# Two small steps of the second head pair's row sums, moved from GpSimd to ScalarE and VectorE

## The chip, the cores and the metric

The kernel runs on one NeuronCore of a Trainium2 chip. The metric is the device time of one execution in microseconds, the median of several runs; lower is better. The engines are named as in the profile: PE is TensorE (PEld its weight loads), DVE is VectorE, ACT is ScalarE, POOL is GpSimd, and SP is SyncE, which issues most of the DMAs. Each engine works through its own instructions in program order, and semaphores hold an instruction until what it reads is there.

## The reference

The reference is attention with rotary embedding, then a top-1 mixture of experts, then a dense layer pair with softplus between. Only the attention is touched by the change. Cut to that:

```python
q_rot, k_rot = (rotate(q), rotate(k))            # 2 batches x 8 heads, 576 positions, 64 wide
scores = scale * np.matmul(q_rot, k_rot.transpose(0, 1, 3, 2))
scores = scores - np.max(scores, axis=-1, keepdims=True)
attn = np.exp(scores)
attn = attn / (np.sum(attn, axis=-1, keepdims=True) + 1e-09)
out = np.matmul(attn, v)
```

The addition of `1e-09` to the row sums is the guard addition of this document.

## The kernel before

The 16 heads of the attention run as 8 pairs, numbered j = 0 to 7 (heads 2j and 2j+1); the second pair is j = 1. A row of a head is a query position. Of the 576 rows of a head four blocks of 128 are full and 64 are left over; the left-over rows of both heads of a pair share one block. So a pair has nine blocks, numbered g = 0 to 8, of which g = 4 is the shared one, and the attention has 72 blocks. The loop at line 753 takes one step t for each block, with j and g from `divmod(t, 9)`.

In a step the order of each engine's work is written by hand (the scheduler is switched off). ACT takes the exponentials of block t, and with them adds up its rows into the tile `rst` of the head (`softmax_exp`, L543). PE transposes block t-1 (L549), multiplies the scores of block t+2 (L533), and does the filling work of the step: the products with v (`pv`, L597 to L599), the transposes that prepare the next pair's q and k (L446 and L450, into `pt`), those of a block's 64 left-over columns (`tail`, L581), and a head's output transposed back (`xout`, L616, into `px`). DVE takes the row maxima of block t+1 (L537) and the low parts of the transposed block t-2 (`ev_lo`, L567). ACT copies the high parts of block t-1 (`ev_hi`, L556). Last in the step comes what was put into the list `late`, the latest entry first. Among it is the second half of `xout`, on DVE: the reciprocal of the row sums (L621), then two products that empty the `px` bank (L623 into `zp`, L628 into `xrow`).

The banks `pt`, `tail`, `px` and `po` come from one PSUM pool with two buffers (`ps_m`, tag "m"). A bank that PE wants to write must have been emptied: the `pt` that follows a `tail` in the first step of a pair takes the bank of the `px` before it.

The row sums of a head go through `ev_lo`. After the shared block (g = 4) the sums of the odd head's left-over rows, which lie in the even head's tile, are copied to the odd head's tile (L562). After g = 4 and after g = 8 the guard is added, for the even and for the odd head, into the tile `rinv` (L572 on GpSimd, or L574 on ScalarE). In the kernel before, pair 0 has these steps on VectorE and ScalarE, and the pairs 1 to 7 have them on GpSimd.

GpSimd does mainly the rotation of the pairs to come. In pair j the generator `rope_gen(j + 2)` gives it, step by step, the products with cosine and sine (L379, L381), sums (L389), and the split of k and of v into high and low parts (L412, L414, L396, L394). The small steps on the row sums stand between these in its queue.

Of the kernel before, what the change touches and what calls it, by code (L numbers as in the profile page):

```python
# [25 lines left out]
P = 128  # L26
# [4 lines left out]
LEFT = S - NC4 * P  # L31
# [59 lines left out]
def f(ap):  # L91
    return ap.bitcast(F32)
# [3 lines left out]
def moe_kernel(ctx: ExitStack, tc: tile.TileContext, q, k, v, emb, tau, w1, w2, w_in, w_out, rope, tab, out):  # L96
    nc = tc.nc
    V, A, G, T, SY = nc.vector, nc.scalar, nc.gpsimd, nc.tensor, nc.sync
# [220 lines left out]
    with actx:  # L319
# [178 lines left out]
        def head(i):  # L498
            if i not in heads:
                heads[i] = dict(a=i % 2, rst=rs[i % 3])  # L500
            return heads[i]

        def columns(hd):

            if 'ph' not in hd:
                hd['ph'], hd['pl'] = (hp.tile([P, 4, S], F32R, tag=n, name=n) for n in ("ph", "pl"))
            return hd
# [7 lines left out]
        def where(t):  # L515

            j, g = divmod(t, 9)
            return j, g, ([(2 * j + g // 5, g % 5)] if g != 4 else [(2 * j, 4), (2 * j + 1, 4)])
# [39 lines left out]
        def ev_lo(t):  # L558
            j, g, hs = where(t)
            tp = tiles.pop(('tp', t))  # L560
            if g == 4:
                (G if j else V).tensor_copy(head(2 * j + 1)['rst'][0:LEFT, 4:5], head(2 * j)['rst'][LEFT:P, 4:5])  # L562
            for x, (i, c) in enumerate(hs):
                w = P // len(hs)
                hd = columns(head(i))
                sl = slice(c * P, c * P + w)
                V.tensor_tensor(hd['pl'][:, :, sl], tp[:, :, x * w:x * w + w], f(hd['ph'][:, :, sl]), op=ALU.subtract)  # L567
            if g in (4, 8):
                hd = head(2 * j + g // 8)
                ri = hd['ri'] = small.tile([P, 5], F32, tag="rinv", name="rinv")  # L570
                if j:
                    G.tensor_scalar(ri, hd['rst'][:, 0:5], 1e-9, None, op0=ALU.add)  # L572
                else:
                    A.activation(ri, hd['rst'][:, 0:5], AF.Copy, bias=1e-9)  # L574
# [178 lines left out]
        for t in range(NS + 5):  # L753
            j, g = divmod(t, 9)
# [54 lines left out]
            if 2 <= t < NS + 2:  # L809
                ev_lo(t - 2)  # L810
# [668 lines left out]
```

## Time and profile before

| | us |
|---|---|
| runs: median (lowest to highest of 3) | 575.5 (575.0 to 577.9) |
| the profiled execution | 576.86 |
| its span, first to last instruction | 575.1 |
| PE busy | 545.2 |
| DVE busy | 447.0 |
| ACT busy | 439.0 |
| POOL busy | 203.3 |

The span is 1.8 us shorter than the time of the profiled execution, which itself is 1.4 us above the median of the runs. The attention takes about the first 187 us, the experts go on to about 365 us, and the dense pair ends the kernel. PE is busy for 95% of the span. The page also gives the clock that TensorE was granted, as a share of full speed, in 40 slices of 14.4 us.

A timeline row reads: start, duration, engine, line, operation, what it writes and reads, its shape, and how often it stands there in a run; in brackets the idle time of the engine ahead of it and what ended this.

### The profile page before, as it was taken

To read this page: it belongs to the slowest core of one execution; us is meant where nothing else is said; L and a number is where in the kernel's file an instruction comes from. 1 tells how busy PE (TensorE), PEld (TensorE's weight loads), DVE (VectorE), ACT (ScalarE), POOL (GpSimd) and SP (SyncE) were. 2 spreads that over 40 slices of the span, in tenths; PEclk is the share of its full clock that TensorE was granted. 3 is DMA by queue.
4 is the path that set the end of the run, shared out by engine and by line. 5 is a ranking of instruction groups with operands and counts; after the bars stand their busy time and mean duration, and the time that the engine had idled before them with its cause. 6 is when DMAs were issued, how large, how long until landed. Compare 5 with 4: busy or idle time off the path is not lost. (4 is left out here: it accounts for less than half of the span.)

```text
span 575.1 us, 10070 instructions
## 1 busy us (share of the span) xinstructions
PE 545.2 (95%) x3361; PEld 478.9 (83%) x3361; DVE 447.0 (78%) x741; ACT 439.0 (76%) x838; POOL 203.3 (35%) x317
## 2 busy tenths in 40 slices
PE   6889899999998899999999999998999999999995
PEld 6789899999888788887777888886889999888994
DVE  5797688787977679989999999687877766787243
ACT  3788688877875599789988998788878877677550
POOL 7999999839931330332222311200000000000033
PEclk9999899999999999999999999999999999999998
DMA  5434100051143635892539895373332222000012
GB/s 142 112 96 121 33 0 2 2 199 58 38 137 146 190 130 166 303 350 77 172 123 319 296 382 196 92 220 108 109 99 85 75 74 75 35 1 1 1 74 91
DMA packets 38631, 70.90 MB, mean 123 GB/s; under 512 B 9506, under 2 KB 25250, under 8 KB 38448
## 3 DMA queue, kind: packets, MB, share of 16 engines
q1 hardware_dynamic: 35600, 62.95, 33.2%
q0 software_dynamic: 2800, 7.09, 3.6%
q8 instruction: 28, 0.46, 0.3%
q10 hardware_dynamic: 176, 0.18, 0.2%
q14 instruction: 27, 0.22, 0.1%
HBM read 91.14 MB, written 8.13 MB: 173 GB/s over the span
## 5 line engine op out<-in xcount | busy, mean ns | idle before, releaser
L970 DVE TENSOR_TENSOR wt<-raw,wt 128x1024 fp32r<-128x1024 f32 x100 | 116.3, 1219 | 5.2 <-ACT wt L966 5.1
L1340 PE MATMUL ph<-yt,wt 128*128 128x320 f32 (+1 forms) x576 | 105.5, 336 | 2.7 <-ACT r__5875 L1352 1.8
L1340 PEld LDWEIGHTS ph<-yt,wt 128*128 128x128 f32 x576 | 93.5, 188 | 12.2 <-ACT r__5875 L1352 2.3
L1387 PE MATMUL po<-wt,g 128*128 128x512 f32 x432 | 103.6, 391 | 0.0
L966 ACT CAST wt<-raw 128x1024 fp32r<-128x1024 f32 x100 | 98.9, 1066 | 5.4 <-DMA raw<-in_moe_w_dram 5.4
L1387 PEld LDWEIGHTS po<-wt,g 128*128 128x128 f32 x432 | 80.4, 188 | 16.7 <-ACT g L1371 0.3
L1034 PE MATMUL py<-wt,ht 128*128 128x512 f32 x312 | 75.7, 395 | 3.6 <-DVE wt L970 3.6
L1404 POOL DMA_INDIRECT out_dram<-acc,otok x9 | 9.6, 1067 | 186.2 <-DVE acc L1401 185.6
L1034 PEld LDWEIGHTS py<-wt,ht 128*128 128x128 f32 x312 | 57.5, 188 | 16.3 <-DVE wt L970 4.9
L1005 PE MATMUL ph<-wt,xt 128*128 128x512 f32 x288 | 69.1, 394 | 0.0
L543 ACT ACTIVATE p<-sc,nm 128x576 f32<-128x576 f32 x72 | 54.0, 750 | 12.5 <-DVE nm L537 11.9
L1005 PEld LDWEIGHTS ph<-wt,xt 128*128 128x128 f32 x288 | 53.1, 188 | 10.6
L537 DVE TENSOR_REDUCE nm<-sc 128x1 f32<-128x576 f32 x72 | 54.1, 753 | 5.5 <-PE sc L533 4.3
L556 ACT CAST ph<-tp 128x512 fp32r<-128x512 f32 (+1 forms) x80 | 42.8, 547 | 12.9 <-PE tp L549 12.5
L533 PE MATMUL sc<-kt,qt 128*128 128x288 f32 x256 | 51.1, 323 | 1.6 <-ACT p L543 1.0
L567 DVE TENSOR_TENSOR pl<-tp,ph 128x512 fp32r<-128x512 f32 (+1 forms) x80 | 49.4, 627 | 0.0
L379 POOL TENSOR_TENSOR t<-qk,ropet 128x256 f32<-128x256 f32 x61 | 43.8, 746 | 11.1 <-DMA qk<-in_q_dram 10.7
L549 PE MATMUL tp<-idf,p 128*128 128x128 f32 x288 | 44.6, 278 | 1.9 <-DVE jz L233 0.6
L1371 ACT CAST g<-e 128x512 fp32r<-128x512 f32 (+2 forms) x33 | 21.6, 658 | 29.7 <-PE po L1387 20.2
L1372 DVE TENSOR_TENSOR g<-e,g 128x512 fp32r<-128x512 f32 (+2 forms) x33 | 24.3, 740 | 23.7 <-ACT g L1371 23.5
L533 PEld LDWEIGHTS sc<-kt,qt 128*128 128x128 f32 x256 | 37.4, 195 | 2.9 <-ACT p L543 1.9
L597 PE MATMUL po<-ph,vs 128*128 128x288 f32 x128 | 36.8, 309 | 2.7 <-DVE p L435 1.5
(245 smaller groups left out, 1002.4 us busy)
## 6 DMA issues: line engine op xcount, KB each, us to landing
raw<-in_moe_w_dram SPq DMA_DIRECT2D x116, 512.0 KB
raw<-in_moe_w_in_dram SPq DMA_DIRECT2D x16, 512.0 KB
raw<-in_moe_w_out_dram SPq DMA_DIRECT2D x16, 512.0 KB
yr<-ys SPq DMA_DIRECT2D x9, 256.5 KB
qk<-in_k_dram SPq DMA_DIRECT2D x8, 256.0 KB
qk<-in_q_dram SPq DMA_DIRECT2D x8, 256.0 KB
vv<-in_v_dram SPq DMA_DIRECT2D x8, 256.0 KB
xs<-xrow SPq DMA_DIRECT2D x1, 1024.0 KB
```

The source lines that it names most:

```text
L379: eng.tensor_tensor(t[:, i, g], x4[:, i, g], ropet[:, m, 0:4].unsqueeze(2).to_broadcast([P, 4, 2, 32]), op=ALU.mult)
L533: T.matmul(sc[:, n, 0:288], lhsT=w, rhs=r, start=(x == 0), stop=(x == len(mm) - 1))
L537: V.tensor_reduce(nm, tiles['sc', t][:, :, 0:288], axis=AX.XY, op=ALU.max, negate=True)
L543: A.activation(p.rearrange("p (n t) -> p n t", n=2), tiles.pop(('sc', t))[:, :, 0:288], AF.Exp, bias=tiles.pop(('nm', t)), accum_out=head( ...
L549: T.transpose(tp[:, x], p[:, x * P:x * P + P], idf)
L567: V.tensor_tensor(hd['pl'][:, :, sl], tp[:, :, x * w:x * w + w], f(hd['ph'][:, :, sl]), op=ALU.subtract)
L966: A.copy(wt[:, 0], raw)
L970: (eng or V).tensor_tensor(wt[:, 1], raw, f(wt[:, 0]), op=ALU.subtract)
L1005: T.matmul(ph[i], lhsT=xt[:, a, c], rhs=wt[:, r, 512 * i:512 * i + 512] if n else wt[r][:, 512 * i:512 * i + 512], start=(c == 0 and a == ...
L1034: T.matmul(py, lhsT=ht[c // 2][:, a, k], rhs=rhs[:, s], start=(c == 0 and r == 0 and a == 0 and s == 0), stop=(c == 3 and r == 1 and a == 1))
L1340: T.matmul(phs[i][:, 0:n1 - n0], lhsT=wt[:, a, k], rhs=yts[p][:, r, k, n0:n1], start=(k == 0 and a == 0 and r == 0), stop=(k == 3 and a == 1))
L1387: T.matmul(outs[i][c], lhsT=g[:, a, c * P:c * P + P], rhs=wt[:, r], start=(first and a == 0 and r == 0), stop=(last and a == 1))
```

## The change

In the two conditions of `ev_lo` the pair number from which the steps go to GpSimd rises by one: pair 1 now has them where pair 0 has them.

```diff
             if g == 4:
-                (G if j else V).tensor_copy(head(2 * j + 1)['rst'][0:LEFT, 4:5], head(2 * j)['rst'][LEFT:P, 4:5])
+                (G if j > 1 else V).tensor_copy(head(2 * j + 1)['rst'][0:LEFT, 4:5], head(2 * j)['rst'][LEFT:P, 4:5])
...
-                if j:
+                if j > 1:
                     G.tensor_scalar(ri, hd['rst'][:, 0:5], 1e-9, None, op0=ALU.add)
                 else:
                     A.activation(ri, hd['rst'][:, 0:5], AF.Copy, bias=1e-9)
```

Three instructions change their engine; PE and SP keep theirs as they were. In the rows below `rs0`, `rs1` and `rs2` are the three tiles of row sums, which the heads take in turn (head 2 has `rs2`, head 3 has `rs0`), and `rinv` is the sums with the guard added.

On POOL, at the end of the split of k for pair 3:

```order
 L412 CAST ks_849<-t1_676 128x9x64
 L414 TENSOR_TENSOR ks_849<-t1_676,ks_849 128x9x64
-L562 COPY rs0_99<-rs2_101 64x1
-L572 TENSOR_SCALAR rinv_877<-rs2_101 128x5
 L396 CAST vs_679<-vv_634 128x4x64
 L394 TENSOR_TENSOR vs_679<-vv_634,vs_679 128x4x64
```

The copy of the last sums and head 2's guard addition no longer stand behind the split of k; head 3's addition, 11 rows further on, goes as well.

On ACT, in step t = 15 (the seventh block of pair 1), for head 2:

```order
 L604 COPY ot0_142<-po_831 128x288
 L434 CAST p4_817<-po_831 64x2x64
+L574 ACTIVATE rinv_877<-rs2_101 128x5
 L556 CAST ph_846<-tp_856 128x4x128
 L543 ACTIVATE p_883,rs0_99<-sc_826,nm_872 128x576
```

Head 2's addition now stands ahead of the copy of the high parts of block 14. Head 3's stands in the same way in step t = 19, between the casts of `qt` and `ph`.

On DVE, in step t = 15:

```order
 L567 TENSOR_TENSOR pl_714<-tp_789,ph_713 128x4x128
 L537 TENSOR_REDUCE nm_872<-sc_826 128x1
+L562 COPY rs0_99<-rs2_101 64x1
 L567 TENSOR_TENSOR pl_714<-tp_821,ph_713 128x4x64
 L567 TENSOR_TENSOR pl_847<-tp_821,ph_846 128x4x64
```

The copy of the last sums now stands between the row maxima of block 16 and the low parts of block 13.

## Rows read from the trace of the kernel before

**Rows 1.** The page: busy time and share of engines; granted clock, tenths, 40 slices.
```profile
PE 545.2 (95%) x3361; PEld 478.9 (83%) x3361; DVE 447.0 (78%) x741; ACT 439.0 (76%) x838; POOL 203.3 (35%) x317
...
PEclk9999899999999999999999999999999999999998
```

**Rows 2.** Stretches: length, each engine's busy time, granted clock, DMA share, GB/s.
```profile
56.00:58.00 2.00, 1.44 (x13) 1.16 (x11) 0.00 (x1) 1.49 (x4) 1.86 (x2) 1.00 0.58 171
58.00:60.00 2.00, 0.39 (x3) 0.42 (x4) 1.29 (x4) 0.29 (x1) 1.76 (x5) 0.94 0.12 26
60.00:62.00 2.00, 2.00 (x11) 2.00 (x10) 1.97 (x4) 1.07 (x2) 1.84 (x5) 0.50 0.00 0
62.00:64.00 2.00, 2.00 (x13) 2.00 (x13) 1.52 (x3) 0.85 (x3) 1.92 (x4) 0.71 0.50 137
```

**Rows 3.** Timeline of DVE around 58 us.
```profile
55.32 0.68 DVE L567 TENSOR_TENSOR pl<-tp,ph 128x512 fp32r<-128x512 f32 x1
58.57 0.19 DVE L621 RECIPROCAL rinv<-rinv 128x5 f32<-128x5 f32 x1 [2.57 <-POOL rinv L572]
...
58.98 0.48 DVE L628 TENSOR_TENSOR xrow<-px,rinv 128x320 f32<-128x320 f32 x1
```

**Rows 4.** Timeline of POOL in the same stretch.
```profile
56.53 1.41 POOL L414 TENSOR_TENSOR ks<-t,ks 128x576 fp32r<-128x576 f32 x1
58.01 0.18 POOL L562 COPY rs<-rs 64x1 f32<-64x1 f32 x1
58.28 0.26 POOL L572 TENSOR_SCALAR rinv<-rs 128x5 f32<-128x5 f32 x1
58.60 0.40 POOL L396 CAST vs<-vv 128x256 fp32r<-128x256 f32 x1
...
63.91 0.23 POOL L572 TENSOR_SCALAR rinv<-rs 128x5 f32<-128x5 f32 x1
```

**Rows 5.** Timeline of PE in the same stretch.
```profile
54.74 1.30 PE L616 MATMUL px<-xm,ot 128*128 128x72 f32 x10
...
56.84 0.60 PE L581 MATMUL tail<-idf,p 128*64 128x128 f32 x4
59.61 0.97 PE L450 MATMUL pt<-idf,qq 128*128 128x128 f32 x4 [2.17 <-DVE xrow L628]
```

**Rows 6.** Stretches from the middle of one pair to the next, columns as in rows 2.
```profile
46.95:70.45 23.50, 21.14 (x162) 20.37 (x161) 16.60 (x31) 16.66 (x42) 22.50 (x36) 0.93 0.28 79
70.45:90.62 20.17, 19.77 (x161) 18.80 (x161) 16.37 (x32) 16.49 (x42) 19.16 (x33) 1.00 0.00 1
90.62:110.82 20.20, 19.82 (x162) 18.85 (x161) 16.38 (x32) 16.48 (x42) 18.34 (x30) 1.00 0.01 2
```

**Rows 7.** Timeline of DVE: the subtraction after block g = 4 of pairs 1 and 2.
```profile
46.95 0.68 DVE L435 TENSOR_TENSOR p<-tail,p 64x512 fp32r<-64x512 f32 x1 [1.72 <-ACT p L434]
...
70.45 0.69 DVE L435 TENSOR_TENSOR p<-tail,p 64x512 fp32r<-64x512 f32 x1 [1.72 <-ACT p L434]
```

**Rows 8.** Timelines of ACT and DVE in pair 0, which has the steps there.
```profile
28.28 0.20 ACT L574 ACTIVATE rinv<-rs 128x5 f32<-128x5 f32 x1
28.38 0.57 ACT L556 CAST ph<-tp 128x512 fp32r<-128x512 f32 x1
...
28.29 0.15 DVE L562 COPY rs<-rs 64x1 f32<-64x1 f32 x1
```

**Rows 9.** Timelines of POOL, DVE and PE: the same place in pair 2.
```profile
75.95 0.23 POOL L572 TENSOR_SCALAR rinv<-rs 128x5 f32<-128x5 f32 x1
...
79.39 0.18 DVE L621 RECIPROCAL rinv<-rinv 128x5 f32<-128x5 f32 x1
...
80.76 0.60 PE L450 MATMUL pt<-idf,qq 128*128 128x128 f32 x4
```

**Rows 10.** Timeline of PE: two later pauses.
```profile
196.75 0.54 PE L984 MATMUL pt<-idr,xg 128*128 128x128 f32 x4 [1.51 <-DMA xg<-xs,idx]
...
390.93 3.03 PE L1340 MATMUL ph<-yt,wt 128*128 128x512 f32 x12 [1.83 <-ACT r__5875 L1352]
```

## The prediction

> **What bounds the kernel now.** I read the page first: PE is busy for 95% of the span and its granted clock is at full speed in nearly all slices, but the fifth slice (57.5 to 71.9 us) shows an 8 [rows 1]. So the first question was what PE lacks in that slice. Cut into stretches of 2 us, it shows PE busy for 1.44 and then 0.39 of 2 us, and right after that a granted clock of 0.50, which is the lower of its two levels (1.2 instead of 2.4 GHz), until about 63 us [rows 2]. The reader is to see two losses there that follow one another: a pause, and then work at half clock.
>
> Next I followed the pause back, engine by engine. PE ends the transposes of `tail` at 57.44 and starts those of `pt` at 59.61, a pause of 2.17 us that is put down to DVE's product L628 [rows 5]; `pt` needs the bank that L628 empties. DVE had ended its work at 56.00 and stood 2.57 us ahead of the reciprocal L621, for POOL's addition L572 [rows 3]. POOL did this addition from 58.28 to 58.54, directly behind the split of k for pair 3 and the copy L562 [rows 4]. DVE started 0.03 us after POOL's end, and what else DVE needs, the `px` products of PE, had ended by 56.04 [rows 5], so the wait is rightly named. The sums themselves had long been there: they belong to block g = 4, and the filling work of that block is seen on DVE at 46.95 [rows 7]. POOL was simply late with its queue.
>
> **What the pause costs in all.** I measure it from pair to pair, between the same instruction of two pairs: the subtraction L435 after block g = 4 starts at 46.95 in pair 1 and at 70.45 in pair 2 [rows 7]. That is 23.50 us, against 20.17 us and 20.20 us in the next two pairs, with practically the same number of instructions, all at full clock [rows 6]. The excess is 23.50 - 20.17 = 3.33 us. Of it 2.17 us are the pause, and the remaining 1.16 us are the half clock after it.
>
> The stretches give the clock's part in another way: at half speed PE ran for 0.24 us (of 58 to 60, from 0.94), 2.00 us, and 1.16 us (of 62 to 64, from 0.71), together 3.40 us [rows 2]. The page "TensorE: Matmul & The Clock Gate" of the Trainium skill (section "HAM oscillation") prices time at the lower clock at one minus the ratio of the clocks, here one half, which would be 1.70 us and a sum of 575.5 - 2.17 - 1.70 + 0.1 = 571.7 us. The pairs bear out only 1.16 us of it, and I go by them, since part of those 3.40 us went to waits that the slow clock hid.
>
> **The change, part by part.**
>
> 1. *The guard addition of head 2 goes to ACT, step 15.* It then stands ahead of a `ph` cast, in the seventh block of pair 1, some 6 us ahead of the reciprocal that needs it. Its price is in pair 0: the addition starts at 28.28 and the next cast at 28.38, so it takes 0.10 us of ACT's queue, although it lasts 0.20 us [rows 8]. Behind it are that cast and the next exponentials, and behind these PE's transposes. PE is busy for 19.77 of 20.17 us in a pair and ACT for 16.49 [rows 6], so ACT has 3.7 us of idle time in a pair to give. Between 0 and 0.20 us; I take 0.
>
> 2. *The guard addition of head 3 goes to ACT, step 19.* The same price, 0.10 us of queue, at the place where PE now stands at half clock. Its reader, the reciprocal of head 3, comes five blocks later, so nobody waits for it. Between 0 and 0.20 us; I take 0.05.
>
> 3. *The copy of the last sums goes to DVE, step 15.* It lasted 0.15 us in pair 0 [rows 8]. Behind it in DVE's queue are the low parts of block 13 and then the maxima of the next block. DVE is busy for 16.37 of 20.17 us in a pair [rows 6]. Its source is old by then, and it adds no wait. Between 0 and 0.15 us; I take 0.05.
>
> 4. *POOL loses three instructions.* The first two are worth 58.60 - 58.01 = 0.59 us of its queue, the third 0.23 us [rows 4], so everything behind it comes 0.82 us earlier. PE waits for nothing of POOL's rotation here, so this gives no time by itself, but it matters for what is late next.
>
> 5. *The wait of DVE goes.* The reciprocal can follow L567 at 56.00. After it L628 starts 0.41 us later (58.57 to 58.98) and lasts 0.48 [rows 3], so the bank is empty at about 56.9. PE ends `tail` at 57.44: no pause is left, and without the pause I see nothing that would lower the clock. The whole 3.33 us go. In pair 2, which has this order without the wait, PE starts `pt` at 80.76 in the same place without any idle time ahead of it [rows 9].
>
> **What is late next.** Pair 2 has the same chain with POOL still in it. There POOL's addition ended at 76.18, and the reciprocal came at 79.39 [rows 9]. With PE and DVE 3.33 us earlier and POOL 0.82 us earlier these become 76.06 and 75.36. So a margin of 0.70 us is left of 3.21 us. PE has another margin: L628 would end 0.41 + 0.48 us after the reciprocal's start, at 80.28, against 80.76 for `pt`, 0.48 us. Both together have to be used up, 1.18 us, until PE pauses again. In the next pairs POOL's share of a pair falls (19.16 and 18.34 us of 20.2 [rows 6]), so pair 2 is the tight one.
>
> **Does the gain reach the end?** From the pause on, each engine follows the blocks of the attention, and what comes after it starts from the results of its last pair. I see no transfer that keeps its old time by itself. So I carry the gain through to the end in full.
>
> **The sum.** 3.33 us off, 0.10 us on: -3.2 us. The profiled execution (576.86 us, with a span of 575.1 and 1.8 outside it) would come to 573.6. Against the median of the runs, 575.5, the forecast is 572.3 us. The bounds of the parts give 575.5 - 3.33 = 572.2 without added costs and 575.5 - 3.33 + 0.55 = 572.7 with all of them; with half a microsecond for the scatter of a median, 571.7 to 573.2. About 0.5% (2.9 us) is what a measurement of this kernel can tell from no change; the forecast lies just beyond that.
>
> **The rivals.**
>
> *The half clock does not stand in every run.* The pause of 2.17 us was followed by the lower clock in this one execution, but pauses of 1.51 and 1.83 us [rows 10] were not (their slices, the 14th and the 28th, read 9 [rows 1]), so it may be a near thing. If the runs mostly kept the full clock, only the pause is there to be gained: 575.5 - 2.17 + 0.1 = 573.4 us. For it: the pause is not far above those without effect. Against: the only execution seen has it, and its time lies among those of the runs. The same page of the Trainium skill ("Part 1: The HAM clock gate") says that the clock's monitor runs free of the kernel's start and that the same kernel therefore slows at different places from run to run; no trace here can show that, with one execution.
>
> *The wait comes back in pair 2, or the gain is lost at the handover to the experts.* If POOL is later than I reckon by over 1.18 us, PE pauses again at about 77.4 us, and each further tenth costs a tenth. At the handover the pause for the gathered rows [rows 10] may lengthen, because the weights' transfers meet the gather at another moment. Either would leave 573.0 to 575.5 us.
>
> *The change does not do what it says*: PE waits at the same place for something else. The release 0.03 us after POOL's end, and DVE idle ahead of it, speak against it. 575.5 us.
>
> *Slower than before.* The one mechanism that I can price: the pause of PE for the gathered rows, 1.51 us at 196.75 [rows 10], lengthens beyond the 2.17 us that brought the half clock, and the first expert then runs at that clock. Lengthened by x it costs x + 1.16 us. Against a gain of 3.2 us it decides from x = 2.1 us on; doubled to some 4.5 us (x = 3.0) it gives 575.5 - 3.2 + 4.2 = 576.5 us. For it: that wait ends with a transfer. Against: the addresses for the gather, the transfer of its rows and PE all come earlier by the same amount.
>
> **How the numbers follow.** The forecast has 0.60, the full clock in most runs 0.14, the return of the wait or the loss at the handover 0.16, no effect 0.04, and slower 0.06. The range goes from 571.3 (below the forecast's own 571.7, towards the sum with the higher price of the clock) to 574.6, which takes in the second case and most of the third. Of the forecast's 0.60 some 0.48 lie below 572.6, and of the others 0.04: faster by over 0.5% 0.52. Slower by over 0.5% needs most of a second pause besides: 0.03. The rest, 0.45, is within 0.5%.
>
> **What would show it.** DVE's reciprocal of head 2 starts right behind L567, at about 56 us, with no idle time put down to POOL. PE has no pause at `pt` at about 57.4, and the clock of 60 to 64 us reads 1.00. The subtractions L435 of pairs 1 and 2 lie 20.2 us apart. ACT shows the two additions at 0.2 us with no wait ahead of them. In pair 2 POOL's addition ends some 0.7 us before the reciprocal. The pauses later on keep their lengths. The prediction is wrong if the pair takes 20.2 us and the end still does not come 3 us earlier, or if the pair does not shorten.

## The result and the profile after

The changed kernel took 581.43 us (median of 14 runs, 578.46 to 586.0) against 575.93 us for the kernel before (14 runs on the same chip): a ratio of 1.0101 with a 95% interval of 1.0078 to 1.0125. It is slower by about 1%, and the forecast of 572.3 us, with its range up to 574.6, was wrong.

| | before | after |
|---|---|---|
| the profiled execution, us | 576.86 | 585.32 |
| its span, us | 575.1 | 583.5 |
| mean granted clock | 0.994 | 0.987 |
| pair 1, from DVE's L435 to that of pair 2, us | 23.50 | 20.15 |
| first gathered rows reach PE (L984), at us | 196.75 | 201.64 |
| the dense pair starts on PE (L1340), at us | 365.73 | 372.59 |

The profiled execution lies 3.9 us above the median of its runs, so its parts add up to more than the median's 5.5 us.

The page shows PE standing still where it did not before, and a clock that is not full in more places. First the busy time and the clock in 40 slices, of after, to be held against [rows 1]:

```profile
PE 549.3 (94%) x3361; PEld 482.1 (83%) x3361; DVE 448.5 (77%) x742; ACT 439.0 (75%) x840; POOL 203.9 (35%) x314
...
PE   7889999999999499999999999998999999999995
...
PEclk9989999999999899999999999998999999999999
```

The slice that the prediction spoke of (the fifth) now reads 9. But the 14th slice (190 to 204 us) has PE at 4 tenths busy, and the third, the 14th and the 28th have a clock of 8 tenths. PE's instructions are the same 3361, so its longer busy time (549.3 against 545.2 us) goes with the lower clock.

**What the change was to do, it did.** The timeline of DVE of after, at the place of [rows 3] (start, duration, engine, line, operation, tiles, shape, count):

```profile
58.01 0.68 DVE L567 TENSOR_TENSOR pl<-tp,ph 128x512 fp32r<-128x512 f32 x1
58.61 0.18 DVE L621 RECIPROCAL rinv<-rinv 128x5 f32<-128x5 f32 x1
...
59.01 0.48 DVE L628 TENSOR_TENSOR xrow<-px,rinv 128x320 f32<-128x320 f32 x1
```

The reciprocal stands right behind L567; the 2.57 us put down to POOL are gone. The timeline of PE of after, at the place of [rows 5]:

```profile
59.55 0.60 PE L581 MATMUL tail<-idf,p 128*64 128x128 f32 x4
59.98 0.60 PE L450 MATMUL pt<-idf,qq 128*128 128x128 f32 x4
```

No pause stands ahead of `pt`. And the stretches from the middle of one pair to the next, of after, as in [rows 6] (length, busy time of PE, PEld, DVE, ACT, POOL, granted clock, DMA share, GB/s):

```profile
49.67:69.82 20.15, 19.63 (x161) 18.79 (x161) 16.52 (x32) 16.65 (x44) 19.61 (x30) 1.00 0.22 65
69.82:89.98 20.16, 19.79 (x162) 18.82 (x161) 16.38 (x31) 16.46 (x42) 19.09 (x32) 1.00 0.01 1
```

Pair 1 is as short as the pairs behind it, at full clock. It gave 23.50 - 20.15 = 3.35 us, where 3.33 us were forecast.

**Where the time went.** The gain was in part gone already, since pair 1 began later: L435 stands at 49.67 instead of 46.95. Two stretches of pair 0, of after:

```profile
32.00:34.00 2.00, 1.24 (x5) 1.24 (x6) 1.94 (x4) 0.58 (x2) 2.00 (x4) 0.67 0.17 30
34.00:36.00 2.00, 2.00 (x11) 1.98 (x10) 1.36 (x3) 0.36 (x2) 1.92 (x5) 0.50 0.70 161
```

PE lacks work and then runs at half clock there, ahead of all that the change touches (the last section shows how this stretch differs from one execution to the next). When pair 1 is done, after is 0.63 us ahead of before all the same (69.82 against 70.45). The large loss comes next, at the handover to the experts. Stretches of 10 us of before, columns as above:

```profile
160.00:170.00 10.00, 9.29 (x77) 8.75 (x77) 7.83 (x17) 7.26 (x18) 4.74 (x11) 1.00 0.34 95
170.00:180.00 10.00, 9.27 (x74) 8.47 (x73) 7.86 (x20) 7.60 (x19) 1.03 (x3) 1.00 0.55 222
...
190.00:200.00 10.00, 8.21 (x116) 7.50 (x117) 6.16 (x22) 4.28 (x6) 4.84 (x4) 1.00 0.68 209
```

And of after:

```profile
160.00:170.00 10.00, 9.29 (x77) 8.76 (x76) 7.68 (x18) 7.19 (x18) 4.61 (x10) 1.00 0.01 2
170.00:180.00 10.00, 9.26 (x74) 8.46 (x74) 7.86 (x18) 6.94 (x18) 0.95 (x2) 1.00 0.00 1
180.00:190.00 10.00, 8.95 (x123) 8.04 (x121) 6.49 (x26) 2.99 (x9) 1.45 (x3) 1.00 0.81 270
190.00:200.00 10.00, 4.34 (x81) 4.05 (x78) 3.83 (x15) 4.03 (x4) 1.85 (x2) 1.00 0.90 324
200.00:210.00 10.00, 8.36 (x40) 7.10 (x41) 5.13 (x7) 5.17 (x8) 3.45 (x4) 0.66 0.28 84
```

The engines do nearly the same from 160 to 180 us, but the DMA engines, which were a third to a half busy before, stand idle. From 180 us on they are nearly full, PE loses more than half of the ten microseconds from 190 on, and the clock falls behind that. Something that was loaded before 180 us is now loaded after it. The timeline of SP's queue tells what; of before:

```profile
161.67 7.02 SPq L943 DMA_DIRECT2D raw<-in_moe_w_dram  x4
168.74 1.60 SPq L956 DMA_DIRECT2D raw<-in_moe_w_dram  x2
179.49 0.59 SPq L170 DMA_DIRECT2D xs<-xrow  x1
```

And of after:

```profile
180.88 3.52 SPq L943 DMA_DIRECT2D raw<-in_moe_w_dram  x4
184.45 0.90 SPq L956 DMA_DIRECT2D raw<-in_moe_w_dram  x2
185.40 0.59 SPq L170 DMA_DIRECT2D xs<-xrow  x1
```

The load of expert 1's first weights (L943, in `fetch_ahead`; six tiles of 512 KB with the two of L956) starts 19.2 us later, and stands directly in front of the last stores of the attention's rows (L170, L171), which the experts' gather reads. What SP waits for ahead of L943 is named in its waits (line waited for: us in total, times, longest), of before and then of after:

```profile
SPq L943 <- DVE xrow L628: 13.4, 1, 13.4
```

```profile
SPq L943 <- DVE xrow L628: 33.3, 1, 33.3
```

Both times it is DVE's product L628, of different heads: in before it is head 12's, in after head 14's, a whole pair later. The load reads nothing that L628 writes. Its target `raw00` lies in memory that the attention's pools have given back, and L628 is the last reader of one of those buffers.

The consequence stands in the timelines of POOL and PE of after; the gather, and the product that takes its rows:

```profile
197.84 1.30 POOL L979 DMA_INDIRECT xg<-xs,idx  x1 [12.27 <-issue]
```

```profile
201.64 0.75 PE L984 MATMUL pt<-idr,xg 128*128 128x128 f32 x4 [7.03 <-DMA xg<-xs,idx]
...
397.75 4.62 PE L1340 MATMUL ph<-yt,wt 128*128 128x512 f32 x12 [1.82 <-ACT r__5875 L1352]
```

PE's pause for the gathered rows is 7.03 us instead of 1.51 [rows 10]. The 12.27 us of POOL ahead of the gather read "issue", that is, no releaser is named there, but the view of the tile `xs` names them as a wait for the stores:

```profile
who waited for it (us, times):
  POOL xg L979: 12.3, 1
```

The balance of the two profiled executions, after minus before: +2.72 us at L435 of pair 1; -3.35 us through pair 1; -0.63 us in all from there to the end of the attention; +4.89 us at the gathered rows (201.64 - 196.75); +6.86 us when the dense pair starts, the first expert having run at half clock in part (0.66 from 200 to 210 us); and +8.4 us at the end, 1.59 us of it from the second row of PE above, where the twelve products took 4.62 us, in part at half clock, in place of 3.03 [rows 10].

### The profile page after: what moved, and what is told of

Its sections match the earlier page's. It is cut to its first block, busy times and chain, and to the rows that moved or that the text cites. A ratio compares the mean times of both kernels' runs of the same rounds, so it can differ in the third digit from the quotient of the medians.

```text
span 583.5 us, 10065 instructions
## 1 busy us (share of the span) xinstructions
PE 549.3 (94%) x3361; PEld 482.1 (83%) x3361; DVE 448.5 (77%) x742; ACT 439.0 (75%) x840; POOL 203.9 (35%) x314
## 5 line engine op out<-in xcount | busy, mean ns | idle before, releaser
L1340 PE MATMUL ph<-yt,wt 128*128 128x320 f32 (+1 forms) x576 | 107.1, 340 | 2.6 <-ACT r__5875 L1352 1.8
L1340 PEld LDWEIGHTS ph<-yt,wt 128*128 128x128 f32 x576 | 94.6, 190 | 12.6 <-ACT r__5875 L1352 2.2
L533 PE MATMUL sc<-kt,qt 128*128 128x288 f32 x256 | 51.0, 322 | 1.8 <-DVE kt L435 1.2
L567 DVE TENSOR_TENSOR pl<-tp,ph 128x512 fp32r<-128x512 f32 (+1 forms) x80 | 49.5, 628 | 0.1
L549 PE MATMUL tp<-idf,p 128*128 128x128 f32 x288 | 44.4, 277 | 2.8 <-DVE est L656 1.0
L533 PEld LDWEIGHTS sc<-kt,qt 128*128 128x128 f32 x256 | 37.3, 194 | 2.8 <-DVE kt L435 1.4
```

What stands on the lines that cost most here:

```text
L533: T.matmul(sc[:, n, 0:288], lhsT=w, rhs=r, start=(x == 0), stop=(x == len(mm) - 1))
L549: T.transpose(tp[:, x], p[:, x * P:x * P + P], idf)
L1340: T.matmul(phs[i][:, 0:n1 - n0], lhsT=wt[:, a, k], rhs=yts[p][:, r, k, n0:n1], start=(k == 0 and a == 0 and r == 0), stop=(k == 3 and a == 1))
```

## Why the load waits for another head

The places of the tiles in the built programs explain it. The tile `raw00` starts at byte 63392 of each partition of SBUF and reaches over the last three of the eight buffers of the pool `small` that hold the sums with the guard added (`rinv`, 32 bytes apart, the first at 63232). Which of the sixteen heads lie in these three:

```
buffer at    before              after
63392        heads 4 and 12      heads 6 and 14
63424        heads 3 and 11      heads 3 and 11
63456        heads 1 and  9      heads 1 and  9
```

Eight buffers serve the heads in an order that the pool sets when the program is built. With the change that order is another one: head 12 moved out from under `raw00` and head 14 moved in. So the load has to wait until DVE has used the sums of head 14. In the built programs this comes from head 3's guard addition alone; head 2's addition and the copy leave the places as they were.

This makes a theory with numbers: the change gains about 3 us in pair 1, and where 96 bytes of row sums lie costs some 8 us or more from the handover on. Its rival is that the steps themselves, on ACT and DVE, bring the loss, and the load only shows it. Eight kernels tell them apart.

## The experiments

**Head 3's addition stays on GpSimd.** The copy and head 2's addition move, as in the change; the places are those of before.

```diff
-                if j > 1:
+                if j > 1 or (j == 1 and g == 8):
                     G.tensor_scalar(ri, hd['rst'][:, 0:5], 1e-9, None, op0=ALU.add)
```

> Only head 3's guard addition goes back to GpSimd; head 2's stays on ScalarE and the copy on VectorE. In this program the sums of head 14 are again kept apart from the place of the experts' first weight tile, as in the kernel before. Place theory (the change moves the sums of heads 6 and 14 to a buffer under that weight tile, so that its load waits for head 14): the load starts near 158 us, the pause for the gathered rows is about 1.5 us, the gain of pair 1 (3.3 us) stays, and the time is 572.6 us. Timing theory (the attention that ends 3 us earlier makes gather and weights collide by itself): the pause is near 7 us and the time about 581 us. Cost theory (the new instructions on ScalarE and VectorE cost the time): two of three are left, so 578 to 581 us.

574.49 us (12 runs) against 576.48 us (21 runs), a ratio of 0.9958 (0.9938 to 0.9978): faster. SP's and PE's timelines:

```profile
159.85 7.09 SPq L943 DMA_DIRECT2D raw<-in_moe_w_dram  x4
```

```profile
194.10 0.54 PE L984 MATMUL pt<-idr,xg 128*128 128x128 f32 x4 [0.50 <-DMA xg<-xs,idx]
```

The load is early, the pause for the gathered rows short, and pair 1 takes 20.17 us. The gain is 2.0 us, not the 3.3 that were expected; in the profiled execution pair 1 begins at 48.77 us, 1.82 us later than in before, with half clock in pair 0 (the last section).

**Head 3's addition alone.** The copy and head 2's addition stay on GpSimd; the places are those of after. The edit, against the change:

```diff
-                (G if j > 1 else V).tensor_copy(head(2 * j + 1)['rst'][0:LEFT, 4:5], head(2 * j)['rst'][LEFT:P, 4:5])
+                (G if j else V).tensor_copy(head(2 * j + 1)['rst'][0:LEFT, 4:5], head(2 * j)['rst'][LEFT:P, 4:5])
...
-                if j > 1:
+                if j > 1 or (j == 1 and g == 4):
```

> Only head 3's guard addition goes to ScalarE; head 2's and the copy stay on GpSimd. In this program the sums of head 14 lie under the first weight tile, as in the changed kernel, while the wait in pair 1 stays. Place theory: no gain, the whole price: the load of the first weights starts near 184 us, the pause for the gathered rows is about 7 us, and the time is 575.9 + 8.8 = about 584.7 us. Timing theory: the attention ends as before, so 575.9 us. Cost theory: one addition of 0.2 us, 576 us.

584.24 us (4 runs), 1.0146 (1.0115 to 1.0176). The load comes at 179.74 us and PE's pause for the rows is 7.11 us. An instruction of 0.20 us on ACT, for which nobody waits, costs 1.5% in this way. The wait of DVE is back in pair 1 too, as it has to be, but smaller; DVE's and PE's timelines:

```profile
58.44 0.19 DVE L621 RECIPROCAL rinv<-rinv 128x5 f32<-128x5 f32 x1 [1.10 <-POOL rinv L572]
```

```profile
59.48 0.63 PE L450 MATMUL pt<-idf,qq 128*128 128x128 f32 x4 [0.70 <-DVE xrow L628]
```

So the loss goes with head 3's step. That could still be the step itself, or the places. The next two runs part these: they fix the places by a table, and swap them.

**The change, with the places of before.** Each head's buffer is named instead of taken from the pool.

```diff
+SLOT = (0, 7, 1, 6, 5, 2, 3, 4, 0, 7, 1, 6, 5, 2, 3, 4)
...
-                ri = hd['ri'] = small.tile([P, 5], F32, tag="rinv", name="rinv")
+                ri = hd['ri'] = rv[SLOT[2 * j + g // 8]]
...
         softmax_max(0)
+        rv = [small.tile([P, 5], F32, name=f"rv{s}", bufs=1) for s in range(8)]
```

> All three instructions moved as in the changed kernel; the eight buffers of the guarded sums are fixed by a table, to the places that the kernel before has them in (heads 4 and 12 under the first weight tile, heads 6 and 14 not). Place theory: 572.5 us, the load near 158 us, a pause of about 1.5 us. Timing theory and cost theory: 581 us as the changed kernel.

572.69 us (10 runs), 0.9948 (0.9927 to 0.997). The load starts at 159.84 us, PE's pause for the rows is 0.69 us, pair 1 takes 20.19 us. With the places kept, the forecast holds in its size. SP's queue:

```profile
159.84 7.00 SPq L945 DMA_DIRECT2D raw<-in_moe_w_dram  x4
```

**The kernel before, with the places of after.** The table is (0, 7, 1, 6, 2, 3, 5, 4) twice; all engines keep their steps.

> All instructions on the engines of the kernel before; only the buffers of the guarded sums are fixed by a table to the places that the changed kernel has them in (heads 6 and 14 under the first weight tile). Place theory: about 584.7 us with the load near 184 us and a pause of about 7 us. Timing theory and cost theory: no difference to the kernel before, 575.9 us.

584.83 us (4 runs), 1.0144 (1.0114 to 1.0174). SP's queue and PE:

```profile
181.40 3.45 SPq L945 DMA_DIRECT2D raw<-in_moe_w_dram  x4
```

```profile
202.31 0.75 PE L986 MATMUL pt<-idr,xg 128*128 128x128 f32 x4 [7.19 <-DMA xg<-xs,idx]
```

(Lines behind the table are shifted by one or two.) No step of the change is in this kernel, and it has the whole loss. The places alone cost 1.0144 here, and 1.0101 / 0.9948 = 1.0154 between the change with its own places and with the old ones. The two parts multiply to what the change as a whole gave: 1.0144 x 0.9948 = 1.0091, measured 1.0101 (1.0078 to 1.0125). The rival falls.

**The kernel before, with a table of its own places.** A control: whether naming the buffers costs or gains something.

> The kernel before in all engines and places; only that the guarded sums' buffers are fixed by the table instead of being drawn from the pool. All theories: the same time as the kernel before, 576 us. A difference of over 1 us would mean that the table itself changes something, and the runs with it would have to be read against this one.

576.2 us (10 runs) against 575.6 us, 1.0014 (0.9997 to 1.0032). The table does nothing that can be told; the load is at 161.86 us, and DVE waits 2.52 us and PE 2.12 us, close to [rows 3, 5].

**The change, with only early heads in those three places.** The second half of the table is (5, 6, 7, 0, 1, 2, 3, 4), so that the heads 8, 9 and 10 are the last there.

> All three instructions moved; the guarded sums' buffers are fixed by a table so that heads 8, 9 and 10 are the last in the three places under the first weight tile. Place theory: that load waits for nothing of VectorE any more, only for GpSimd's split, and starts some microseconds earlier than with the old places (near 156 us); the handover is no tighter than with the old places, so 572 to 573 us. If an earlier load is worth more by itself, under 571 us.

573.19 us (12 runs), 0.9955 (0.9938 to 0.9973). The load starts at 147.84 us (near 156 us was expected), 12 us earlier than with the places of before, and PE's pause for the rows is 0.79 us. SP's queue:

```profile
147.84 16.11 SPq L945 DMA_DIRECT2D raw<-in_moe_w_dram  x4
```

Only the first tile is really earlier. SP then waits 14.4 us in one piece for GpSimd's split (`part`, L493), and the fourth tile goes out at 163.5 us against 166.4 with the places of before, in an execution whose attention is itself 2.8 us ahead (L435 of pair 1 at 45.55 against 48.37). So the gain is no larger than with the places of before, and whether all six tiles fetched earlier would bring more is not shown.

**The change, with the weight tiles moved up.** The pad below them grows by 96 bytes, past the three buffers.

```diff
-        wr.tile([P, 528], F32, name="below")
+        wr.tile([P, 552], F32, name="below")
```

> All three instructions moved and the guarded sums left to the pool, as in the changed kernel; the pad below the experts' weight tiles grows from 528 to 552 words, so that no guarded sums lie under them. Place theory: the same cure in another way, 572 to 574 us, the load near 156 us. If the table of the earlier runs and not the place made the difference, 581 us.

572.11 us (5 runs), 0.9927 (0.9903 to 0.9951): the lowest ratio of all, though its interval overlaps with those of the other kernels with an early load. The sums lie here where they lie in after; only the overlap with the weight tile is gone, and with it the loss. So it is this overlap that costs, and not the places as such. SP's queue, PE, and pair 1:

```profile
148.78 16.11 SPq L943 DMA_DIRECT2D raw<-in_moe_w_dram  x4
```

```profile
192.13 0.54 PE L984 MATMUL pt<-idr,xg 128*128 128x128 f32 x4 [0.60 <-DMA xg<-xs,idx]
```

```profile
46.59:66.78 20.19, 19.66 (x161) 18.83 (x161) 16.52 (x32) 16.66 (x44) 19.57 (x29) 1.00 0.32 93
```

Its profiled execution is 4.7 us shorter than that of before, and this is accounted for: -0.36 us at L435 of pair 1, -3.31 us in pair 1 (23.50 to 20.19), -0.91 us in the pause for the rows (1.51 to 0.60), together -4.58; the dense pair starts 4.70 us earlier (361.03 against 365.73), and the span ends 4.7 us earlier (570.4 against 575.1). The gain of pair 1 is carried to the end in full where nothing stands in the way. (The 0.91 us of the pause may be in part scatter: with no step changed, the kernel before with its places by table paused 0.85 us. The medians differ by 3.5 us.)

**The change, with the stores ahead of the late load.** If the loss is only that six weight tiles go out in front of the rows' stores, it should shrink when the order in SP's queue is turned round.

```diff
-        fetch_ahead()
         x_store(1, 0, 6 * D)
...
         x_store(1, 6 * D, DM)
+        fetch_ahead()
```

> The changed kernel with its places as they are; only the issue of six weight tiles on SyncE is put behind the two stores of the second batch's rows. The load is then even later (near 188 us). If the price of the late load is that the rows' stores, and with them the gather, stand behind 3 MB of weights: the gather starts near 190 us again and the pause for the gathered rows is back to 0.5 to 2 us; what is left is that the first expert's second layer and the second expert wait for weights, 574 to 578 us. If the late weights themselves hold PE: 581 us or more.

584.29 us (4 runs), 1.0132 (1.0089 to 1.0176): nothing is won, and the 574 to 578 us of this expectation are missed. The gather does come earlier; POOL, then PE, then ACT:

```profile
188.13 1.31 POOL L979 DMA_INDIRECT xg<-xs,idx  x1 [5.18 <-DVE sel L285]
```

```profile
195.57 0.54 PE L984 MATMUL pt<-idr,xg 128*128 128x128 f32 x4 [3.59 <-DMA xg<-xs,idx]
...
202.38 5.01 PE L1005 MATMUL ph<-part,xt 128*128 128x512 f32 x12 [5.42 <-ACT xt L988]
```

```profile
197.60 2.13 ACT L966 CAST wt<-raw 128x1024 fp32r<-128x1024 f32 x2 [13.34 <-issue]
```

The pause for the rows shrinks from 7.03 to 3.59 us, but behind it PE waits 5.42 us for ACT. ACT's queue has the casts of the weight tiles ahead of the cast of the gathered rows, and the weights now come last: ACT idles 13.34 us ahead of these casts ("issue" again; they read the tiles that L943 and L956 load). So the price lies in the late load as such and not in its place ahead of the stores; 3 MB that were fetched under the attention must be fetched while PE has little else to do, in one order or the other.

All of them at a glance; the ratios are to the kernel before in the same comparison:

| kernel | ratio (95%) | load L943 starts, us | pause for the rows, us | pair 1, us |
|---|---|---|---|---|
| after | 1.0101 (1.0078 to 1.0125) | 180.88 | 7.03 | 20.15 |
| head 3's addition stays | 0.9958 (0.9938 to 0.9978) | 159.85 | 0.50 | 20.17 |
| head 3's addition alone | 1.0146 (1.0115 to 1.0176) | 179.74 | 7.11 | 20.43 |
| after, places of before | 0.9948 (0.9927 to 0.997) | 159.84 | 0.69 | 20.19 |
| before, places of after | 1.0144 (1.0114 to 1.0174) | 181.40 | 7.19 | 25.17 |
| before, its places by table | 1.0014 (0.9997 to 1.0032) | 161.86 | 0.85 | 23.45 |
| after, early heads there | 0.9955 (0.9938 to 0.9973) | 147.84 | 0.79 | 20.19 |
| after, weight tiles moved up | 0.9927 (0.9903 to 0.9951) | 148.78 | 0.60 | 20.19 |
| after, stores first | 1.0132 (1.0089 to 1.0176) | 185.40 | 3.59 | 20.20 |

## Why the prediction was wrong

**What bounds the kernel at that place: right.** The pause was POOL's lateness and nothing else: with the addition on ACT it is gone in every kernel that has it so.

**The price of the pause and the clock together, 3.33 us: right for the execution seen, but it is a price of that execution.** Kernels that keep the wait took 23.50, 23.45, 25.17 and 20.43 us for pair 1, and those without it 20.15 to 20.20. So the same wait cost between 0.3 and 5 us. The rows say how. POOL's addition ends at nearly the same time whatever the attention does (the reciprocal behind it came at 58.57, 58.44, 58.76 and 58.78 us), while the attention reaches this place sooner or later, depending on what happened in pair 0: in the same order of kernels (before, head 3's addition alone, before with the places of after, before with its places by table) L435 stands at 46.95, 48.29, 45.41 and 47.21 us. The earlier it comes, the longer the wait; the longest, of the kernel before with the places of after, on DVE:

```profile
58.76 0.19 DVE L622 RECIPROCAL rv<-rv 128x5 f32<-128x5 f32 x1 [4.30 <-POOL rv L573]
```

The gains of the four kernels with an early load and without the wait, 0.9927 to 0.9958, are 4.2 to 2.4 us and so lie around the forecast's 3.2.

**The split of the 3.33 us: wrong.** The prediction took the 2.17 us of the pause as carried in full and left 1.16 us for the half clock. The kernel with head 3's addition alone has a pause of 0.70 us at full clock, and its pair 1 is only 20.43 - 20.17 = 0.26 us longer: what a short pause costs is in part taken from waits that PE has a little later without it. The clock's price can be read from one and the same work of PE, from `pt` to the transposes L549 behind the next products with v. These transposes, in the kernel with head 3's addition alone and in before:

```profile
62.10 0.60 PE L549 MATMUL tp<-idf,p 128*128 128x128 f32 x4
```

```profile
63.83 0.60 PE L549 MATMUL tp<-idf,p 128*128 128x128 f32 x4
```

From `pt` at 59.48 and at 59.61 that is 2.62 us at full clock and 4.22 us in before (4.22 with its places by table, 4.11 with the places of after). So the half clock cost 1.60 us, and the pause the other 1.73. The 1.70 us, an estimate by the Trainium skill's page "TensorE: Matmul & The Clock Gate" (section "HAM oscillation"), lie close to the 1.60 us measured. The sum itself is not touched by this, since it uses the 3.33 us as a whole.

**The parts 1 to 3: right.** The additions take 0.21 and 0.20 us on ACT without a wait ahead of them, the copy 0.15 us on DVE, and pair 1 is no longer than pairs 2 and 3 were. Nothing that can be seen is added.

**Part 4 and what is late next: right in that PE does not pause, but the margin is not safe.** In pair 2 POOL's addition ends at 74.60 us in the kernel with the weight tiles moved up, and the reciprocal comes at 75.75: a margin of 1.15 us where 0.70 us were forecast, because POOL came 1.58 us earlier (from 76.18) and not only 0.82. Why by so much was not followed up. In after, with its late pair 0, the margin is 3.95 us. It is smaller where the attention comes earlier: in the kernel with early heads in the three places, where L435 of pair 1 stands at 45.55 us, it is used up, and DVE waits for POOL in pair 2:

```profile
75.11 0.19 DVE L622 RECIPROCAL rv<-rv 128x5 f32<-128x5 f32 x1 [0.34 <-POOL rv L573]
```

PE has no idle time there yet, and pair 2 takes 20.16 us.

**"Does the gain reach the end?": the step that failed.** It said that no transfer keeps its old time by itself, and put the loss on the way to the end at nothing. That holds for what this load reads, but its weights go into memory that others have used, and so the load waits for the last of these others too. The change altered who that is: head 14 in place of head 12. The load came at 180.88 in place of 161.67 us and the pause for the gathered rows grew from 1.51 to 7.03 us; the places alone, with no step moved, cost 1.0144 (1.0114 to 1.0174), more than the gain. I looked at the change as one of times and queues, and the order of the instructions shows no more than this. It moves a buffer as well. The trace of before had the sign: SP waits 13.4 us for a product of the attention (`xrow`, L628) before it loads weights, which have nothing to do with `xrow`. A wait of which the data give no account points to memory, and every change to the pools concerned has to be weighed against it.

**The rival "slower": the right place, the wrong cause and size.** It let the pause for the gathered rows grow by x, to be paid with x + 1.16 us. With the measured x = 7.03 - 1.51 = 5.5 us its formula gives 575.5 - 3.2 + 5.5 + 1.16 = 579.0 us, near the lowest of the runs (578.46). I had doubled the pause, to x = 3.0, as a far end, and gave the case 0.06, since everything behind the attention was to come earlier "by the same amount". This argument fell with the step above. The second rival named the same place too, with the weights' transfers meeting the gather, but let it take back no more than the gain (573.0 to 575.5 us).

**The rival "the half clock does not stand in every run": not borne out at this place.** In all three executions whose pause at `pt` was over 2 us (2.17, 2.12 and 3.90 us) the half clock followed it; behind the pause of 0.70 us the pair ran at full clock. In other places the clock does fall in some executions and not in others, and costs or spares one to two microseconds; the last section has the rows. Its price of 2.17 us for the pause alone goes with the split above: 1.73 us would have been left to gain.

## What to carry to other kernels

Where a pool decides which buffer a tile gets, a step on another engine can change the places of tiles, and with them which instruction a much later load has to wait for; here 96 bytes of pad were worth 1.0101 / 0.9927 = 1.0175 (the ratios of two comparisons). Before a small edit near such a pool, look through the waits for loads that wait on results they do not read, and compare the places of the tiles in the two built programs as well as the order of instructions. A gain at a wait on an engine that keeps its own time is to be priced over several executions: here the same wait cost 0.26 us in one and 5.00 us in another.

## What was not expected of the hardware

**A product on DVE stands still until one on GpSimd ends.** Where in pair 0 an execution loses time is set by DVE's product L394 (a low part of v, of two operands in SBUF), which stands ahead of what PE waits for next (`kt`, L435). Its duration runs from 0.43 to 1.66 us for the same shape. DVE and then POOL, of the change with early heads in the three places (lines shifted by one):

```profile
29.33 0.43 DVE L395 TENSOR_TENSOR vs<-vv,vs 128x256 fp32r<-128x256 f32 x1
```

```profile
29.33 1.71 POOL L390 TENSOR_TENSOR qq<-t,t 128x576 f32<-128x576 f32 x1
```

And the same two of after:

```profile
30.83 1.56 DVE L394 TENSOR_TENSOR vs<-vv,vs 128x256 fp32r<-128x256 f32 x1
```

```profile
30.70 1.41 POOL L389 TENSOR_TENSOR qq<-t,t 128x576 f32<-128x576 f32 x1
```

In the first, DVE came with POOL and took 0.43 us, and POOL's sum took 1.71 us instead of 1.41. In the second, POOL had begun 0.13 us before, and DVE ended at 32.39, 0.28 us after POOL (32.11). The same 0.28 us stands in all eight executions in which POOL's sum was under way first (before: 31.13 after 30.85; weight tiles moved up: 30.80 after 30.52). The page "SBUF — State Buffer" of the Trainium skill (section "Who interferes with whom") says that a Vector instruction with two SBUF inputs contends with a GpSimd instruction that reads SBUF, as its second input comes through a read interface that both use, and that issue order decides which of the two waits; the traces agree, with these numbers. So in pair 0 the two executions differ in when DVE came upon POOL's two sums: 0.69 us into the first of them in before (30.13 against 29.44), 0.13 us into the second in after. The code up to there is the same in both.

**The same pause is followed by half clock in one execution and not in another.** Behind the late L394 PE pauses a second time in pair 0 (at L533, after 1.47 us at L448 in every execution). In six executions that pause was 1.20 to 1.30 us, and in four of them the half clock followed (after, and the first three experiments), with L435 of pair 1 at 48.29 to 49.67; in two it did not (the stores first; before by table), with L435 at 46.97 and 47.21. Where the pause was 0.65 us or less the clock never fell, and L435 came at 45.41 to 46.95. So two causes that are outside the change move this point by some 4 us (45.41 to 49.67) and, since POOL keeps its own time, the wait that the change removes. In the same way a pause of 1.82 us in the dense pair was followed by 4.62 us for twelve products in after, but here, in the kernel before with the places of after, by 3.04 us:

```profile
398.71 3.04 PE L1342 MATMUL ph<-yt,wt 128*128 128x512 f32 x12 [1.82 <-ACT r__5867 L1354]
```

The page "TensorE: Matmul & The Clock Gate" of the Trainium skill ("Part 1: The HAM clock gate"), which the prediction named, says that the point at which the clock changes varies from run to run of one kernel. The ten traces are of ten kernels, but with the same instructions of PE in pair 0, and they agree; so do the 24 runs of the kernel before in one comparison, whose mean granted clock lies between 0.987 and 0.996.

**What stays open.** That the pool's order of buffers turns on head 3's addition was read off the built programs; why it does was not traced back to the pool's rule. Why DVE comes to L394 at different times (29.06 to 30.83 us) was not looked into, nor why the clock fell in four of the six executions and not in the other two; of each kernel there is one profiled execution, so how often its runs have the one or the other is not known.
